# Moving the second half of a weight load from the sync queue to the ACT queue in the opening of a gated linear-attention and SwiGLU kernel

## The chip, the cores and the metric

The kernel runs on one core of one Trainium2 chip. The metric is the device time of a whole execution in microseconds; the span in a profile, from its first to its last instruction, is 1.7 us shorter.

Names: PE is TensorE's matmul, PEld its weight load, ACT ScalarE, DVE VectorE, POOL GpSimd, SP the sync engine, whose queue issues most DMAs. A q behind a name (ACTq, SPq) marks an entry of that engine's sequencer, such as the issue of a DMA.

## The reference, cut to what matters

```python
x = A_x                                       # 1 x 2048 x 512, bf16
g = sigmoid((x * gate_w).sum(-1, keepdims=True))
qkv = x @ wqkv                                # 512 x 1536: q, k, v; 32 heads of 16
pq, pk = phi(q), phi(k)                       # phi(t) = where(t > 0, t + 1, exp(t)) + 1e-6
kv, z = sum_s pk v, sum_s pk                  # per head, over ALL tokens
a = ((pq @ kv) / (pq . z + 1e-6)) @ wo
b = (silu(x @ w1) * (x @ w3)) @ w2            # 512 -> 1376 -> 512
out = g * a + (1 - g) * b
```

kv and z are sums over all tokens, so the kernel starts with k of all 16 token tiles, for which it needs wk and x transposed.

## The kernel before

The opening: x's first two token tiles come as rows and are transposed by PE; tiles 2 and 3 and all later ones come by transposing DMAs. wk (512 x 512) comes in two halves of 256 KB: chunks 0 and 1 of its rows, and chunks 2 and 3.

```python
dq = nc.sync
dq.dma_start(out=x_sb[:, 0:TF, :], in_=x_first)                                    # tiles 0, 1
nc.scalar.dma_start(out=wk_sb[:, 0:2, :], in_=wqkv_r[:, 0:2, D : 2 * D])           # first half
dq.dma_start(out=wk_sb[:, 2:4, :], in_=wqkv_r[:, 2:4, D : 2 * D])                  # second half
pre = consts.tile([1, 1], FP32, name="pre")
nc.scalar.activation(out=pre[:], in_=..., func=ACT.Exp)          # brings the table load with it
dq.dma_start(out=xT[:, :, TF * P : TB], in_=x2d[TF * P : TB, :], transpose=True)   # tiles 2, 3
for tb in range(1, NTB):
    dq.dma_start(out=xT[:, :, ...], in_=x2d[...], transpose=True)
    dq.dma_start(out=x_sb[:, x_ts, :], in_=x_r[:, x_ts, :])
# ... the other weights, all on the sync queue
emit_warm(TB, TB, TB, TB, TB, TB, P, P, P)      # 9 idle matmuls until x lands
emit_xT(0); emit_xT(1)                          # 8 transposes on PE; copies on DVE and ACT
for kc, t in ((0, 0), (1, 0), (0, 1), (1, 1), (2, 0), (3, 0)):
    emit_k_mm(k0[t], t, kc)                     # chunk kc of wk, token tile t
emit_k_phi(k0[0], 0)
for t in range(1, TPB):                         # the rest of tile 1, then tiles 2 and 3
    for kc in range(2 if t == 1 else 0, KC):
        emit_k_mm(k0[t], t, kc)
    emit_k_phi(k0[t], t)
# ... k of the other tiles, x^T pk, q, the FFN and the output: PE without a pause
```

The order of PE's work is fixed by the program. "Chunk 2" below is the fifth k matmul, the first to read wk's second half; "tile 2" is the ninth, the first to read the transposing load.

## Time and profile before

| | kernel before |
|---|---|
| time, median of 3 | 178.72 us (178.37 to 178.73) |
| span of the profiled execution | 176.2 us |
| PE busy, share of the chain that ended last | 98%, 96% |
| first half of wk: issue, landing | 0.80, 4.46 us (ACT queue) |
| second half of wk: issue, landing | 1.27, 5.29 us (sync queue) |
| transposing load of tiles 2 and 3: issue, landing | 1.73, 6.24 us (sync queue) |
| chunk 2 starts, tile 2 starts | 5.38, 6.28 us |

The table reads as follows. PE is the bound and runs from its first k matmul to its end with next to no idle time, so the time is set by when that run begins, by waits in its first few matmuls, and by what follows its end. The lines behind this, and how long chunk 2 and tile 2 wait for their data, are in the prediction.

### The profile page before, as it was taken

To read this page: it belongs to the slowest core of one execution; us is meant where nothing else is said; L and a number is where in the kernel's file an instruction comes from. 1 tells how busy PE (TensorE), PEld (TensorE's weight loads), DVE (VectorE), ACT (ScalarE), POOL (GpSimd) and SP (SyncE) were. 2 spreads that over 40 slices of the span, in tenths; PEclk is the share of its full clock that TensorE was granted. 3 is DMA by queue.
4 is the path that set the end of the run, shared out by engine and by line. 5 is a ranking of instruction groups with operands and counts; after the bars stand their busy time and mean duration, and the time that the engine had idled before them with its cause. 6 is when DMAs were issued, how large, how long until landed. Compare 5 with 4: busy or idle time off the path is not lost.

```text
span 176.2 us, 2619 instructions
## 1 busy us (share of the span) xinstructions
PE 172.6 (98%) x946; PEld 82.7 (47%) x946; DVE 117.5 (67%) x204; ACT 65.3 (37%) x123; POOL 67.0 (38%) x100
## 2 busy tenths in 40 slices
PE   7999999999999999999999999999999999999994
PEld 3444444464445454444454544444545444444463
DVE  0596857899998646697875466978754669776000
ACT  3624224475524333324243332333434323341222
POOL 7297655789028323282003232820032329100000
PEclk9999999999999999999999999999999999999999
DMA  4999989961003611126000101230002022300002
GB/s 164 241 281 222 266 249 364 355 197 24 9 0 81 50 40 34 37 61 91 0 0 7 60 18 51 57 79 2 0 11 67 7 67 55 65 0 4 30 30 60
DMA packets 30380, 15.14 MB, mean 86 GB/s; under 512 B 20928, under 2 KB 30240, under 8 KB 30368
## 3 DMA queue, kind: packets, MB, share of 16 engines
q1 hardware_dynamic: 29952, 14.67, 32.5%
q10 hardware_dynamic: 416, 0.31, 0.5%
q8 instruction: 7, 0.11, 0.3%
q14 instruction: 5, 0.04, 0.1%
HBM read 8.42 MB, written 2.10 MB: 60 GB/s over the span
## 4 chain that ended last, share of the span: by engine, by line
PE 96%; DMA 2%; DVE 0%; issue 0%
PE o_ps L383 20%; PE up_ps L341 20%; PE gate_ps L333 19%; PE o_ps L374 8%; PE q_ps L224 8%; PE XP L211 8%; PE k_ps L191 6%; PE r_ps L248 3%; PE k L191 2%; DMA wk_sb<-in_A_wqkv_dram 2%; PE o_ps L378 2%; PE gate L333 0%; PE kvT_ps L465 0%; PE W_ps L489 0%; DVE o_last L392 0%; PE gate L319 0%
## 5 line engine op out<-in xcount | busy, mean ns | idle before, releaser
L341 PE MATMUL up_ps<-xT,w_sb 128*128 128x512 bf16 x160 | 41.1, 379 | 0.0
L333 PE MATMUL gate_ps<-xT,w_sb 128*128 128x512 bf16 x156 | 40.0, 379 | 0.0
L232 POOL TENSOR_TENSOR qz<-pq,z_sb 128x512 f32<-128x512 bf16 x16 | 18.4, 1161 | 54.5 <-DVE pq L152 54.5
L346 ACT ACTIVATE th<-gate_ps 128x512 bf16<-128x512 f32 x39 | 23.3, 597 | 38.8 <-PE gate_ps L333 38.4
L383 PE MATMUL o_ps<-w_sb,hT 128*128 128x512 bf16 (+3 forms) x180 | 37.5, 355 | 0.0
L348 DVE SCALAR_TENSOR_TENSOR gs<-th,gate_ps 128x512 bf16<-128x512 bf16 x39 | 26.6, 683 | 5.9 <-ACT th L346 5.6
L353 DVE TENSOR_TENSOR hT<-up_ps,gs 128x512 bf16<-128x512 f32 x40 | 27.6, 691 | 3.5
L149 DVE TENSOR_SCALAR phi_m<-phi_e 128x512 bf16<-128x512 bf16 x32 | 13.6, 424 | 21.2 <-ACT phi_e L147 21.1
L383 PEld LDWEIGHTS <-hT 128*128 128x128 bf16 x180 | 16.8, 98 | 17.8
L301 POOL TENSOR_TENSOR pqn<-pq,rden 128x256 bf16<-128x256 bf16 x32 | 19.0, 625 | 15.9 <-DVE rden L292 14.8
L341 PEld LDWEIGHTS <-w_sb 128*128 128x128 bf16 x160 | 15.7, 98 | 18.9
L333 PEld LDWEIGHTS <-w_sb 128*128 128x128 bf16 x159 | 15.4, 98 | 18.5 <-issue 0.2
L388 ACT ACTIVATE o_out<-o_ps,omg 128x512 bf16<-128x512 f32 x15 | 10.3, 687 | 29.0 <-PE o_ps L383 26.3
L201 POOL TENSOR_TENSOR pks<-pks,pk_sb 128x512 f32<-128x512 f32 x15 | 17.5, 1164 | 7.4 <-DVE pk_sb L152 6.7
L374 PE MATMUL o_ps<-W_sb,pqT 128*128 128x512 bf16 (+3 forms) x72 | 16.8, 355 | 0.0
L224 PE MATMUL q_ps<-wq_sb,xT 128*128 128x512 bf16 x64 | 16.4, 379 | 0.0
L211 PE MATMUL XP<-pk_sb,x_sb 128*128 128x512 bf16 x64 | 16.3, 379 | 0.0
L235 DVE TENSOR_REDUCE den<-qz 128x32 f32<-128x512 f32 x16 | 11.0, 685 | 7.9 <-POOL qz L232 7.8
L147 ACT ACTIVATE phi_e<-k_ps 128x512 bf16<-128x512 f32 x12 | 7.2, 597 | 14.4 <-PE k_ps L191 14.4
L147 ACT ACTIVATE phi_e<-q_ps 128x512 bf16<-128x512 f32 x16 | 9.6, 597 | 7.8 <-PE q_ps L224 7.8
L191 PE MATMUL k_ps<-wk_sb,xT 128*128 128x512 bf16 x48 | 12.3, 379 | 0.0
L152 DVE SCALAR_TENSOR_TENSOR pq<-q_ps,phi_m 128x512 bf16<-128x512 f32 x16 | 11.1, 691 | 0.5
(66 smaller groups left out, 119.2 us busy)
## 6 DMA issues: line engine op xcount, KB each, us to landing
w_sb<-in_B_w_dram SPq DMA_DIRECT2D x4, 640.0 KB, 7.1
out_dram<-o_out SPq DMA_DIRECT2D x15, 128.0 KB, 1.7
w_sb<-in_B_w_dram SPq DMA_DIRECT2D x1, 1280.0 KB, 12.7
x_sb<-in_A_x_dram SPq DMA_DIRECT2D x2, 512.0 KB, 5.5
x_sb<-in_A_x_dram SPq DMA_DIRECT2D x1, 768.0 KB, 5.2
wq_sb<-in_A_wqkv_dram SPq DMA_DIRECT2D x1, 512.0 KB, 7.0
wv_sb<-in_A_wqkv_dram SPq DMA_DIRECT2D x1, 512.0 KB, 5.5
wo_sb<-in_A_wo_dram SPq DMA_DIRECT2D x1, 512.0 KB, 9.9
```

The source lines that it names most:

```text
L191: nc.tensor.matmul(k_ps[:], lhsT=xT[:, kc, t * P : (t + 1) * P], rhs=wk_sb[:, kc, :], start=(kc == 0), stop=(kc == KC - 1),)
L211: nc.tensor.matmul(XP_ps[dc][:], lhsT=x_sb[:, t, dc * P : (dc + 1) * P], rhs=pk_sb[:, t, :], start=(t == 0), stop=(t == NT - 1),)
L224: nc.tensor.matmul(q_ps[:], lhsT=xT[:, kc, ts_tok], rhs=wq_sb[:, kc, :], start=(kc == 0), stop=(kc == KC - 1),)
L232: nc.gpsimd.tensor_tensor(out=qz[:], in0=st[tb, "pq"][:, tt, :], in1=z_sb[:], op=ALU.mult)
L301: nc.gpsimd.tensor_tensor(out=pqn[:].rearrange("p (i c e) -> p c i e", i=NG, c=KC)[:, :, :, dsl], in0=st[tb, "pq"][:, tt, :].rearrange("p ...
L333: nc.tensor.matmul(gate_ps[:], lhsT=w1_sb[:, kc, fsl], rhs=xT[:, kc, tok_sl], start=(kc == 0), stop=(kc == KC - 1),)
L341: nc.tensor.matmul(up_ps[:], lhsT=w3_sb[:, kc, fsl], rhs=xT[:, kc, tok_sl], start=(kc == 0), stop=(kc == KC - 1),)
L346: nc.scalar.activation(out=th[:], in_=gate_ps[:], func=ACT.Tanh, scale=0.5)
L348: nc.vector.scalar_tensor_tensor(out=gs[:], in0=th[:], scalar=1.0, in1=gate_ps[:], op0=ALU.add, op1=ALU.mult)
L353: nc.vector.tensor_tensor(out=st[tb, "hT"][:, fc, :], in0=up_ps[:], in1=gs[:], op=ALU.mult)
L374: nc.tensor.matmul(o_ps[:], lhsT=st[tb, "pqT"][:, c, tsl], rhs=W_sb[:, c, a:b], start=(c == 0), stop=False,)
L383: nc.tensor.matmul(o_ps[:], lhsT=st[tb, "hT"][:, fc, tsl], rhs=w2_sb[:, fc, a:b], start=False, stop=(fc == FC - 1),)
```

## The change

Intent: the sync queue should not spend its second place on wk. wk's second half goes out on the ACT queue right behind its first half, ahead of the activation table's load, and the sync queue goes on at once with the transposing load, for which PE waits at tile 2.

```diff
     nc.scalar.dma_start(out=wk_sb[:, 0:2, :], in_=wqkv_r[:, 0:2, D : 2 * D])
-    dq.dma_start(out=wk_sb[:, 2:4, :], in_=wqkv_r[:, 2:4, D : 2 * D])
+    nc.scalar.dma_start(out=wk_sb[:, 2:4, :], in_=wqkv_r[:, 2:4, D : 2 * D])
     pre = consts.tile([1, 1], FP32, name="pre")
     nc.scalar.activation(out=pre[:], in_=nc.const_aps.tensor(0.0, [1, 1], FP32), func=ACT.Exp)
     dq.dma_start(
```

In the compiled program nothing else moves: PE, DVE and POOL have the same instructions in the same order, SP one fewer, ACT one more.

## The prediction

> **What bounds the kernel now.** I read the page's busy times and chain first, then the chain of the first 12 us in order of time, then the timeline of each engine there, then the DMA queues in short windows.
>
> ```profile
> PE 172.6 (98%) x946; PEld 82.7 (47%) x946; DVE 117.5 (67%) x204; ACT 65.3 (37%) x123; POOL 67.0 (38%) x100
> ...
> PE 96%; DMA 2%; DVE 0%; issue 0%
> ```
>
> TensorE is the bound: 172.6 of a span of 176.2 us, and 96% of the chain that ended last. The sums over one long window say how tight it is (columns: PE, PEld, DVE, ACT, POOL, each busy us and count, then clock, DMA share, GB/s):
>
> ```profile
> 4.51:173.60 169.09, 169.07 (x929) 81.12 (x929) 116.82 (x202) 63.60 (x121) 63.45 (x85) 1.00 0.33 85
> ```
>
> From its first k matmul to its last output matmul PE is idle for 0.02 us of 169.09, at full clock. (Matmul ends are modelled, so a short stall can hide in this sum; I look for those below.) There is nothing to win after the opening, and a delay before or in the first matmuls moves the end by as much. So the change is decided by the first 6.3 us. The chain there (start, us, what):
>
> ```profile
> 0.80 3.66 DMA wk_sb<-in_A_wqkv_dram
> 4.46 0.04 issue
> 4.51 3.67 PE k L191 x16
> ```
>
> It starts with the first half of wk, landing at 0.80 + 3.66 = 4.46. The 16 matmuls take 3.67 us, where 16 at the later pace (4 in 0.86 us, 0.216 each) would take 3.45. Part of the rest is the long end of the last one, and part a wait. The timeline of the weight loads shows which:
>
> ```profile
> 3.83 0.45 PEld L181 LDWEIGHTS <-x_sb 128*128 128x128 bf16 x8 [0.25 <-DMA x_sb<-in_A_x_dram]
> 4.50 1.41 PEld L191 LDWEIGHTS <-xT 128*128 128x128 bf16 x8 [0.22 <-DVE xT L186]
> 6.28 0.11 PEld L191 LDWEIGHTS <-xT 128*128 128x128 bf16 x2 [0.36 <-DMA xT<-in_A_x_dram]
> ```
>
> The third line is the wait that the change aims at: the matmuls of token tile 2 begin at 6.28, released by the transposing load. The matmul before started at 6.03, so the pace allowed 6.03 + 0.216 = 6.245. The wait is worth 0.03 to 0.04 us of PE's time; the 0.36 in the brackets is idle time of the weight loader, which idles 0.12 us before every load here anyway. The second line has no DMA wait between its eight loads: the matmuls of chunk 2, the first readers of wk's second half, start at 5.38, four paces after 4.51. That half was issued at 1.27 and took 4.0 us (its row of landings), so it landed at about 5.29, and PE reads it about 0.04 us after a landing (4.46 to 4.51). So it has under 0.1 us of slack.
>
> The issues on both queues and what ACT does meanwhile:
>
> ```profile
> 0.80 0.46 ACTq L86 DMA_DIRECT2D wk_sb<-in_A_wqkv_dram  x1
> 1.29 1.28 ACT L89 ACT_TABLE_LOAD   x1 [1.29 <-PEq L531]
> 4.27 0.38 ACT L188 ACTIVATE xT<-xTp 128x256 bf16<-128x256 bf16 x1 [1.48 <-PE xTp L181]
> ```
>
> ```profile
> 0.81 0.40 SPq L85 DMA_DIRECT2D x_sb<-in_A_x_dram  x1
> 1.27 0.41 SPq L87 DMA_DIRECT2D wk_sb<-in_A_wqkv_dram  x1
> 1.73 1.32 SPq L90 DMA_TRANSPOSE xT<-in_A_x_dram  x1
> ```
>
> Last, the queue table (packets, MB, share of 16 engines) of 2.9 to 3.7, of 4.1 to 4.45 and of 4.6 to 5.6 us; q10 is ACT's queue, q1 the sync engine's:
>
> ```profile
> q10 hardware_dynamic: 189, 0.19, 72.0%
> q1 hardware_dynamic: 56, 0.08, 27.4%
> ```
>
> ```profile
> q1 hardware_dynamic: 131, 0.13, 107.8%
> ```
>
> ```profile
> q1 hardware_dynamic: 1105, 0.28, 126.6%
> ```
>
> They give the cost of a packet: wk's 1 KB ones 1.078 x 16 x 0.35 us / 131 = 46 ns, the transposing load's 256 B ones 1.266 x 16 x 1.0 us / 1105 = 18 ns. A half of wk is 256 packets, 16 per DMA engine, 0.74 us; the transposing load is 256 KB, 1024 packets, 64 per engine, 1.17 us. Up to 2.9 us q1 alone moved packets (88 of them, x), then q10 for the most part, then q1 alone. So today x, wk's first half, its second half and the transposing load are served one after another, though the first two were issued at the same moment on two queues.
>
> **What the Trainium skill says.** "DMA: Bandwidth & Descriptors", section "Issuing engines are not separate DMA queues": DMAs of all engines run on the same 16 DMA engines and interleave; issuing from several saves the sequencer's time only. The trace agrees: the engines are full from 2.5 to beyond 6 us, so the order of service matters, not the number of queues. The same page, "Queues, rings and completion order", has each DMA engine go round its queues packet by packet. The trace does not show it for x and wk's first half, which hardly overlap. "Perfetto Trace Analysis", section "DMA Instruction — HWDGE (DVE, Sync)", gives a reason: the descriptor generator is one block that an issuing sequencer locks for exclusive use, and the recorded issue includes the wait for the lock. The trace fits loosely: ACT's issue took 0.46 us beside x's, the same transfer alone on SP 0.41. "TensorE: Matmul & The Clock Gate", part 1: the clock falls after about 3.4 us of idle time; a stall of 1 us should cost itself and no more (no row of this trace has one).
>
> **The change part by part.** Both programs hold the same instructions; the order on PE, DVE and POOL is the same, the waits too. One DMA moves from second on the sync queue to second on ACT's.
>
> Sync queue: 0.41 us and its gap go, so the transposing load is issued at 1.27 instead of 1.73, and all behind it 0.46 us earlier. Only the 0.04 us wait at 6.28 can be won. The next transposing load lands 4.9 us after 3.10 at the earliest (7.97), and its readers start at 8.88, so it is hidden already.
>
> ACT: the issue adds some 0.46 us; the table load goes from 1.29 to 1.75 and ends at 3.03, the dummy Exp (0.20) at 3.24. ACT's first real work starts at 4.27, so 1.03 us of slack is left. Cost 0.
>
> DMA engines: the same bytes, in another order. wk's second half and the transposing load are now ready within some 0.05 us of each other, around 1.27, and SP is free first (1.21 against 1.26). The first half of wk is asked for before both and should keep its place. What counts is the second half's landing, with under 0.1 us of slack.
>
> **The rivals.**
> (a) Served as before, wk's half ahead: the generator takes it between pieces of the long transposing issue. PE wins the wait at 6.28: -0.04 us. For it: only 0.05 us separates the two requests, and the 1.32 us issue may be many pieces.
> (b) Interleaved packet by packet: each of the 16 packets of wk waits for one of 18 ns, 16 x 18 = 0.29 us. The half lands at about 5.58 and chunk 2 starts at 5.62 instead of 5.38: +0.24 us. The wait at 6.28 is then hidden, so +0.2. If the first half is caught too, it comes 0.29 us later and the two delays add up to 0.4 or so. For it: two queues, one set of engines, and the skill's round robin.
> (c) The transposing load takes the generator for its whole 1.32 us, or its packets go first: the second half takes the last place and lands where the transposing load lands now, 1.73 + 4.5 = 6.23, or up to 5.29 + 1.17 = 6.46. Chunk 2 starts at 6.27 to 6.50: +0.9 to +1.1 us. ACT would be held till 2.59 and its table load would end near 4.3, with its first copy some 0.25 us late, which hides under the same stall (the copy is read at 5.38 at the earliest). For it: strict one-after-another service today, and SP being free first. Against it: ACT's issue beside x's grew by only 0.05 us.
> A fourth, that the earlier sync queue brings the later weights sooner, makes nothing: PE waits for no DMA after 6.28.
>
> **Range and chances.** The weights are a 0.3, b 0.4, c 0.3: 0.3 x (-0.04) + 0.4 x 0.3 + 0.3 x 0.95 = +0.39 us. The three runs before average 178.6 (178.37, 178.72, 178.73), so 179.0. The range is from 178.4, case (a) with a low run, to 179.8, case (c) with a usual one. 2% is 3.6 us, over three times the worst rival; 0.98 for within 2%, and slower a little likelier than faster.
>
> **What would show it.** In the changed profile the table load starts near 1.75 and ACT's first copy still at 4.27 (or near 4.5 under c). The transposing issue starts near 1.27. If the weight loads of the first k matmuls break at chunk 2 with a wait on wk, (b) or (c) is right, and its length tells which; then no wait is left on the transposing load. If chunk 2 still starts four paces after the first matmul and tile 2 follows in pace, it is (a). The landing of wk's first half, 3.7 us after issue, should hold within 0.1; if it grows the transposing load already mixes with that half. Wrong altogether would be an ACT copy that ends the wait at 5.38, or any idle time on PE after 6.5 us.

## The result, and the profile after

| | before | changed |
|---|---|---|
| median | 178.72 us (6 runs, 177.99 to 179.20) | 178.43 us (6 runs, 178.21 to 178.77) |
| ratio, 95% interval | | 0.999 (0.9965 to 1.0014) |

A ratio here is the mean time of one kernel's fast runs over that of the other's fast runs of the same rounds, so not quite the ratio of the medians quoted. The interval holds anything from 0.6 us won to 0.25 us lost.

The ACT and sync queues of the changed kernel (start, us, what), to set beside the issues of before:

```profile
0.80 0.47 ACTq L86 DMA_DIRECT2D wk_sb<-in_A_wqkv_dram  x1
1.30 0.50 ACTq L87 DMA_DIRECT2D wk_sb<-in_A_wqkv_dram  x1
1.82 1.28 ACT L89 ACT_TABLE_LOAD   x1 [1.82 <-issue]
3.12 0.20 ACT L89 ACTIVATE pre<-const-float32-0.0 1x1 f32<-1x1 f32 x1
4.35 0.81 ACT L188 ACTIVATE xT<-xTp 128x256 bf16<-128x256 bf16 x2 [1.03 <-PE xTp L181]
```

```profile
1.27 1.33 SPq L90 DMA_TRANSPOSE xT<-in_A_x_dram  x1
2.66 3.35 SPq L94 DMA_TRANSPOSE xT<-in_A_x_dram  x1
```

The intent was met at the issue: the transposing load goes out at 1.27 instead of 1.73, 0.03 us ahead of wk's second half. The table load moves by 0.53 us and ACT still idles 1.03 us before its first real work. The landings of that load, first in the kernel before, then in the changed one:

```profile
L90 SPq DMA_TRANSPOSE xT<-in_A_x_dram x1: 1324/1324/1324, 1.7 to 1.7; - x1
...
DMA to landing us min/median/max: 4.5/4.5/4.5
```

```profile
L90 SPq DMA_TRANSPOSE xT<-in_A_x_dram x1: 1335/1335/1335, 1.3 to 1.3; - x1
...
DMA to landing us min/median/max: 5.1/5.1/5.1
```

Issued 0.46 us earlier, it takes 0.6 us longer: it lands at 6.36 us, no earlier than before. What the DMA engines did in the meantime stands in the queue table of 3.75 to 4.25 us of the changed kernel (queue, packets, MB, share of 16 engines; q10 is ACT's queue, q1 the sync queue):

```profile
q10 hardware_dynamic: 178, 0.17, 106.2%
q1 hardware_dynamic: 1, 0.00, 0.2%
```

The engines are full with wk's second half, and the transposing load has moved one packet. The half went first although it was asked for last, by 0.03 us. In the 0.35 us after this window both queues move packets (78 of ACT's, 158 of the sync queue's). Then the weight loads of the opening, to set beside those of before:

```profile
3.69 0.78 PEld L181 LDWEIGHTS <-x_sb 128*128 128x128 bf16 x8
4.48 0.20 PEld L191 LDWEIGHTS <-xT 128*128 128x128 bf16 x2
4.96 0.15 PEld L191 LDWEIGHTS <-xT 128*128 128x128 bf16 x1 [0.28 <-DVE xT L186]
5.34 2.69 PEld L191 LDWEIGHTS <-xT 128*128 128x128 bf16 x13 [0.23 <-issue]
```

No DMA wait is left among them. But the reason isn't the change: here the loads take 0.15 us and stand 0.43 apart until 5.3 us, and the eight transposes take 0.78 instead of 0.45 us. PE ran at half its pace until then, while in the profile of before it had the full pace from 3.5 us on. Running late, it came to tile 2 at 6.42 and found its data there. So these two profiles can't be compared by their waits, and the experiments first had to deal with that.

One more line of each profile matters, the closing entries of the ACT queue (duration in ns, min/median/max; first and last start), before and changed:

```profile
L542 ACTq DRAIN  x2: 8/80/153, 174.0 to 175.8; - x2
```

```profile
L542 ACTq DRAIN  x2: 122/137/152, 174.4 to 176.4; - x2
```

The last drain takes 122 instead of 8 ns, and starts 2.7 instead of 2.4 us after PE's last weight load. From that weight load to the end of the span it is 2.83 us before and 3.03 in the changed kernel.

### The profile page after: what moved, and what is told of

It is laid out like the page before. It is cut to its first block, busy times and chain, and to the rows that moved or that the text cites. A ratio compares the mean times of both kernels' runs of the same rounds, so it can differ in the third digit from the quotient of the medians.

```text
span 176.7 us, 2603 instructions
## 1 busy us (share of the span) xinstructions
PE 172.1 (97%) x930; PEld 83.3 (47%) x946; DVE 117.5 (67%) x204; ACT 65.5 (37%) x123; POOL 67.1 (38%) x100
## 4 chain that ended last, share of the span: by engine, by line
PE 97%; issue 1%; DVE 0%
PE up_ps L341 20%; PE o_ps L383 19%; PE gate_ps L333 19%; PE o_ps L374 8%; PE q_ps L224 8%; PE XP L211 8%; PE k_ps L191 6%; PE r_ps L248 3%; PE k L191 2%; PE o_ps L378 2%; PE warm L168 2%; PE xTp L181 0%; PE gate L333 0%; PE kvT_ps L465 0%; PE W_ps L489 0%
```

## The experiments

Twelve kernels ran, in three sets of four, each set on one chip together with runs of the kernel before.

### 1. The kernel before against itself, and the changed kernel again

No edit. Both give another profile of the opening.

> The kernel before, unchanged, against itself. Theory O (the change does nothing, its 0.1% is scatter): ratio within 0.25% of 1, and runs of two kinds, with a recorded clock of 1.000 and of about 0.998, the second longer by 0.3 to 0.4 us (in the changed kernel's six runs: mean span 176.6 against 176.9 us). Theory G (the change wins a real 0.3 us): this kernel's runs agree with its own within 0.1 us and show no such two kinds. In the profile both expect the first half of wk to land at 4.2 to 4.6, the second half at 5.2 to 5.4 and the transposing load at 6.1 to 6.4 us.

> The changed kernel again. Theory O: ratio 0.998 to 1.002, the second half of wk lands at 5.2 to 5.4 us and the transposing load at 6.2 to 6.4 though it is issued near 1.27, so its issue to landing is about 5.0 us instead of 4.5. Theory G: ratio at or below 0.998 with the interval clear of 1, and the transposing load lands before 6.1 us.

Measured: the kernel before against itself 0.9977 (0.9943 to 1.0011), the changed kernel 1.0009 (0.9975 to 1.0044). So the 0.1% of the first result is less than what a kernel differs from itself. The recorded clock is not the mark of a kind of run that I expected: spans of 177.0 and of 176.2 both come with 1.000. The pace of the weight loads is a better one. In this second profile of the kernel before they are:

```profile
3.72 0.77 PEld L181 LDWEIGHTS <-x_sb 128*128 128x128 bf16 x8
4.50 0.20 PEld L191 LDWEIGHTS <-xT 128*128 128x128 bf16 x2
4.98 0.15 PEld L191 LDWEIGHTS <-xT 128*128 128x128 bf16 x1 [0.28 <-DVE xT L186]
5.41 0.15 PEld L191 LDWEIGHTS <-xT 128*128 128x128 bf16 x1 [0.28 <-issue]
5.83 0.15 PEld L191 LDWEIGHTS <-xT 128*128 128x128 bf16 x1 [0.28 <-issue]
6.26 0.15 PEld L191 LDWEIGHTS <-xT 128*128 128x128 bf16 x1 [0.28 <-issue]
6.69 1.20 PEld L191 LDWEIGHTS <-xT 128*128 128x128 bf16 x6 [0.28 <-issue]
```

One load each 0.43 us up to 6.7, then the full pace, and the span is 177.2 us. The four profiles so far give the full pace from 3.5, 5.3, 6.1 and 6.9 us on and spans of 176.2, 176.7, 177.1 and 177.2 us, in the same order, whichever of the two kernels it was. A microsecond at half pace costs up to half a microsecond of PE's work, less what PE would have waited for a landing anyway. "TensorE: Matmul & The Clock Gate" of the Trainium skill, part 1, says that the clock's monitor works in windows of about 3.4 us that don't start with the kernel, so that the moment varies from run to run; that fits.

The landings: the transposing load at 6.42 us in the kernel before and 6.14 in the changed one, so over two profiles each the means are 6.33 and 6.25 us, with 0.2 us between two executions of one kernel. wk's second half: 5.31 and 5.01. Two expectations for the changed kernel were missed: 6.2 to 6.4 for the transposing load by 0.06 us, and 5.2 to 5.4 for the half by 0.2. No gain of 0.46 us is there, and none of 0.3 us in the time.

### 2. The transposing load ahead of wk's second half on the sync queue

```diff
-    dq.dma_start(out=wk_sb[:, 2:4, :], in_=wqkv_r[:, 2:4, D : 2 * D])
 ...
     dq.dma_start(out=xT[:, :, TF * P : TB], in_=x2d[TF * P : TB, :], transpose=True)
+    dq.dma_start(out=wk_sb[:, 2:4, :], in_=wqkv_r[:, 2:4, D : 2 * D])
```

> Both loads on the sync queue, the transposing load ahead of wk's second half: this makes certain what rival (c) of the prediction supposed. Expected if the queue serves strictly in order and PE passes a late landing on to the end: the half lands at 6.2 to 6.5 us, the weight loads of chunk 2 wait about 0.8 to 1.1 us, time +0.8 to +1.1 us (ratio 1.0045 to 1.006). If a later clock rise or another wait already covers it: under +0.4 us. If the 1 KB packets overtake the 256 B ones on one queue: landing before 5.6 and a ratio of 1.

Measured: ratio 1.0048 (1.0016 to 1.0079), +0.86 us. The sync queue, and the row of the half that now comes second:

```profile
1.26 1.33 SPq L89 DMA_TRANSPOSE xT<-in_A_x_dram  x1
2.65 0.56 SPq L92 DMA_DIRECT2D wk_sb<-in_A_wqkv_dram  x1
```

```profile
  PE k L191: 1.3, 1
...
DMA to landing us min/median/max: 4.0/4.0/4.0
```

The half lands at 2.65 + 4.0 = 6.66 us, later than expected, because its issue has to wait for the 1.33 us of the other and its packets come slowly; PE waits 1.3 us for it, once. A late landing does pass on to the end, as the prediction's rival (c) had it. The same run answers the main question. The transposing load was issued at 1.26, as in the changed kernel, and landed at 5.30 instead of 6.14 to 6.36. Its queue table of 3.75 to 4.25 us:

```profile
q1 hardware_dynamic: 521, 0.13, 124.5%
q10 hardware_dynamic: 8, 0.00, 2.8%
```

In the stretch in which it moved one packet in the changed kernel it moves 521 packets here. So what held it back in the changed kernel was wk's second half on the other queue; experiment 4, which takes that half away, agrees. Where it was held back, at the DMA engines or earlier, where the descriptors of the transfers are made, no run tells apart: its first packet comes at 3.4 us here, with wk's first half still under way, and at 4.2 us in the changed kernel.

The half itself crawls here. Its 256 packets take from 4.5 to 6.2 us, 1.7 us, where the prediction's estimate for the half alone is 0.74. They share the one queue with packets of two transposing loads (4.45 to 6.2 us, both kinds together; wk's are 256 of the 779):

```profile
q1 hardware_dynamic: 779, 0.38, 113.3%
```

That is 0.38 MB in 1.75 us, about 217 GB/s, while the engines count as 113% busy.

### 3. wk's second half on ACT behind the table load

```diff
-    nc.scalar.dma_start(out=wk_sb[:, 2:4, :], in_=wqkv_r[:, 2:4, D : 2 * D])
     pre = consts.tile([1, 1], FP32, name="pre")
     nc.scalar.activation(out=pre[:], in_=..., func=ACT.Exp)
+    nc.scalar.dma_start(out=wk_sb[:, 2:4, :], in_=wqkv_r[:, 2:4, D : 2 * D])
```

> wk's second half on ACT behind the table load and the dummy Exp, issued near 2.8 us, well after the transposing load's issue at 1.27. Theory F (one generator, the transfers served in the order in which their requests reach it): the half comes behind the whole transposing load and lands at 6.2 to 6.6, time +0.8 to +1.2 us. Theory R (the DMA engines go round the two queues packet by packet): the half's 16 packets per engine alternate with the transposing load's, it lands 3.0 to 3.3 us after issue, at 5.8 to 6.1, and the transposing load at 6.2 to 6.4; time +0.4 to +0.7 us.

Measured: ratio 1.000 (0.9964 to 1.0036). It tested something else than I meant:

```profile
1.29 1.28 ACT L88 ACT_TABLE_LOAD   x1 [1.29 <-PEq L531]
1.36 0.43 ACTq L89 DMA_DIRECT2D wk_sb<-in_A_wqkv_dram  x1
```

The DMA goes out at 1.36 us, 0.07 us into the table load that stands before it in the program: ACT's sequencer issues it while the engine is still loading. So the place ahead of the table's load, which the change speaks of, is worth 0.06 us of issue time. The half landed at 1.36 + 4.1 = 5.45 us and the transposing load at 6.26, so the first half microsecond of reordering is given back here too. In the window of 3.75 to 4.25 us the transposing load moved 28 packets instead of 1. The half's request came 0.09 instead of 0.03 us after its own; that this made the difference isn't shown.

To put the half truly behind the table load, the dummy Exp then wrote an element of wk that the DMA overwrites, so that the DMA has to wait for it (edit against the run before):

```diff
-    pre = consts.tile([1, 1], FP32, name="pre")
-    nc.scalar.activation(out=pre[:], in_=..., func=ACT.Exp)
+    nc.scalar.activation(out=wk_sb[0:1, 2, 0:1], in_=..., func=ACT.Exp)
     nc.scalar.dma_start(out=wk_sb[:, 2:4, :], in_=wqkv_r[:, 2:4, D : 2 * D])
```

> Mends the run before this set: wk's second half truly behind the table load, because the dummy Exp writes a byte that it overwrites; issued near 2.8 us, 1.5 us after the transposing load. Theory F (served in order of request): lands at 6.2 to 6.7, PE waits at chunk 2 in every run, ratio 1.004 to 1.006 like the swap on the sync queue. Theory R (packet by packet between the two queues): lands at 5.8 to 6.1, ratio 1.001 to 1.004. The transposing load lands near 5.3 under F, at 5.6 or later under R.

Measured: two fast runs of 179.76 and 180.53 us (ratio 1.010, 1.006 to 1.0139), and four slow, up to 186.26. Both theories fall short. The profiled execution is one of the slow ones; the row of the half's issue at 2.83 us reads:

```profile
  PE k L192: 4.4, 1
...
DMA to landing us min/median/max: 8.0/8.0/8.0
```

The half took 8.0 us to land. Its packets ran beside the second transposing load (1024 packets for two tiles, twice that for four), and the two together moved little. Sums of that run (columns PE, PEld, DVE, ACT, POOL, then clock, DMA share, GB/s):

```profile
4.00:5.00 1.00, 1.00 (x9) 0.71 (x8) 0.58 (x2) 0.61 (x2) 0.62 (x2) 1.00 1.12 252
5.00:6.00 1.00, 1.00 (x4) 0.40 (x3) 0.00 (x0) 0.15 (x1) 0.00 (x0) 1.00 1.20 125
6.00:7.00 1.00, 0.41 (x2) 0.00 (x0) 0.00 (x0) 0.00 (x0) 0.00 (x0) 1.00 0.98 111
...
9.00:10.00 1.00, 0.00 (x0) 0.00 (x0) 0.00 (x0) 0.00 (x0) 0.00 (x0) 0.83 1.28 206
10.00:11.00 1.00, 0.17 (x1) 0.10 (x1) 0.00 (x0) 0.00 (x0) 0.00 (x0) 0.50 1.03 186
```

111 to 125 GB/s where the opening of the kernel before has 270 to 375, with the engines counted as busy as ever. While PE idled, the granted clock fell too (1.00, 0.83, 0.50), which goes with this run's counting as slow. The fast runs show that time is lost in every run (1.4 and 2.1 us over the median of before); how long the half crawls in those isn't shown, since only a slow one was profiled. Why a plain load and transposing ones slow each other like this stays open; experiment 2 has a milder case on one queue, so two queues aren't needed for it.

### 4. Without wk's second half (a wrong result)

```diff
-    dq.dma_start(out=wk_sb[:, 2:4, :], in_=wqkv_r[:, 2:4, D : 2 * D])
 ...
-            k_ps[:], lhsT=xT[:, kc, t * P : (t + 1) * P], rhs=wk_sb[:, kc, :],
+            k_ps[:], lhsT=xT[:, kc, t * P : (t + 1) * P], rhs=wk_sb[:, kc % 2, :],
```

> A wrong result on purpose: wk's second half is not loaded, chunks 2 and 3 read the first half. What it is worth to have its 256 KB out of the way. If the transposing load waits for the engines only because that half is ahead of it: it lands 0.7 to 1.0 us earlier (at 5.2 to 5.7) and PE never waits for it. Time: at most 0.1 us won when the clock rises early (PE is then bound by its start at 4.3 to 4.5), ratio 0.998 to 1.001. If the transposing load has a fixed delay of its own it lands at 6.1 to 6.4 as before.

Measured: ratio 0.9991 (0.9966 to 1.0017), relative error 0.027 as intended. The row of the transposing load's landing:

```profile
L89 SPq DMA_TRANSPOSE xT<-in_A_x_dram x1: 1313/1313/1313, 1.3 to 1.3; - x1
...
DMA to landing us min/median/max: 4.2/4.2/4.2
```

Issued at 1.26, it lands at 5.51: with those 256 KB out of the way it comes 0.6 to 0.9 us sooner. And still the time moves by less than the scatter. This bounds what an earlier landing of these two loads could win: the interval leaves at most 0.6 us, the wait at tile 2 in the first profile was worth 0.04 us, and in the other three profiles so far PE isn't even there yet when the load lands.

### 5. The opening held back until the clock is up

To see effects of 0.1 us the scatter had to go. In this pair five memsets on DVE (about 5.6 us) come first; one more writes an element of x and of wk, for which the first DMA on either queue has to wait. PE gets 19 idle matmuls instead of 9, the last four of them at 7.4 us, so that its clock is up and stays up. The two held-back kernels differ from each other in the change alone. (The compiler's scheduling is switched off for SP, ACT and DVE here, in both.)

```diff
+    for _ in range(5):
+        nc.vector.memset(hold[:], 0.0)                          # 128 x 1024 fp32
+    nc.vector.memset(xw_sb[0:1, 0 : NT + 1 : NT, 0:1], 0.0)     # x and wk are one tile here
+    nc.vector.memset(late_r[:], 1.0)
     dq.dma_start(out=x_sb[:, 0:TF, :], in_=x_first)
 ...
-    emit_warm(TB, TB, TB, TB, TB, TB, P, P, P)
+    emit_warm(*[TB] * 15)
+    warm_r = late_r[:]
+    emit_warm(TB, TB, TB, TB)
```

> The kernel before with its whole opening (all DMA issues) held back about 5.6 us by five memsets on VectorE, and PE kept busy meanwhile, so that its clock has risen before x lands. Theory K (the scatter of 1.5 us between runs comes from the moment at which the PE clock rises, 3.5 to 6.9 us into the span in the profiles so far): all matmuls of the opening run at 0.216 us, and the runs' spans lie within 0.4 us of each other instead of 176.0 to 177.7. If the scatter has another cause: they spread by over 1 us as before. Time +4.5 to +6.5 us over the kernel before in either case. Landings counted from the issue of x as in the kernel before: second half of wk 4.4 to 4.6, transposing load 5.3 to 5.7 us.

> The changed kernel held back in the same way; the only difference from the run above is the queue of wk's second half. Here the opening is bound by the transfers, so the change shows undiluted. Theory O (no effect: the half is served first on either queue): mean span within 0.1 us of the run above, the transposing load lands within 0.15 us of it counted from the issue of x. Theory L (in runs with an early clock rise the change costs 0.2 us: the shortest spans so far are 176.4 to 176.5 of the changed kernel against 176.0 to 176.3): mean span 0.1 to 0.3 us longer, with a longer wait on the transposing load or on wk. Theory G (a gain): 0.04 us or more shorter with no wait on the transposing load.

| held back | time of the runs, us | spans, us |
|---|---|---|
| kernel before | 183.76, 183.81, 183.82, 183.88 | 182.0 to 182.2, mean 182.10 |
| changed kernel | 184.03, 184.09, 184.13, 184.15, 184.19 | 182.3 to 182.5, mean 182.38 |

The scatter falls from 1.5 us to 0.12 and 0.16 us (0.2 to 0.6 in the three held-back kernels of the next set), so theory K holds for the most part: nearly all of it came from the moment at which PE's clock rises. And the two kernels separate: 184.118 against 183.817 us in the mean, 0.30 us or 0.16% more for the changed kernel, without overlap. The opening of the held-back kernel before, then of the changed one:

```profile
10.46 1.41 PEld L201 LDWEIGHTS <-xT 128*128 128x128 bf16 x8 [0.22 <-DVE xT L196]
12.19 0.76 PEld L201 LDWEIGHTS <-xT 128*128 128x128 bf16 x5 [0.32 <-DMA xT<-in_A_x_dram]
```

```profile
10.15 0.80 PEld L201 LDWEIGHTS <-xT 128*128 128x128 bf16 x5 [0.22 <-DVE xT L196]
11.31 0.53 PEld L201 LDWEIGHTS <-xT 128*128 128x128 bf16 x3 [0.36 <-issue]
12.25 0.76 PEld L201 LDWEIGHTS <-xT 128*128 128x128 bf16 x5 [0.41 <-DMA xT<-in_A_x_dram]
```

In the changed kernel x and wk's first half landed earlier in this execution (9.44 and 10.17 against 9.75 and 10.40 us), PE began earlier, waited for wk's second half (landed at 11.27) and again for the transposing load (12.21). Tile 2 starts at 12.25 against 12.19, a difference of 0.07 us. In the three held-back kernels of the next set it starts at 12.27 (before's order), 12.75 and 12.19 us (changed order), so 0.07 us is within the scatter between executions. That 0.07 us remains up to PE's last weight load (179.33 against 179.27), so PE lost nothing in between. But the spans of these two executions are 182.35 and 182.10. The other 0.18 us come after PE's end: from the last weight load to the end it is 3.02 us against 2.84. Looking back, that holds for every profile so far. Of the five profiles without a second load on ACT's queue four have 2.83 to 2.84 us (the one without wk's half has 2.91); all five with it have 3.01 to 3.03. The line that goes with it is the closing drain on ACT's queue, shown above for the first pair. For the held-back kernel before and the changed one it reads:

```profile
L552 ACTq DRAIN  x2: 8/80/152, 179.9 to 181.7; - x2
```

```profile
L552 ACTq DRAIN  x2: 121/137/153, 180.0 to 182.0; - x2
```

### 6. Is it the DMA or the instruction?

A second DMA on ACT's queue also makes ACT's stream of instructions one longer: 195 instead of 194 in the compiled program. Three held-back kernels tell the two apart, and one that is not held back. One instruction fewer, by moving an eviction of the third block from ACT to DVE:

```diff
+        if (tb, half) == (2, 1):
+            nc.vector.tensor_copy(out=upr[:], in_=r_ps[:, :, FR:NR])
+        else:
-        nc.scalar.activation(out=upr[:], in_=r_ps[:, :, FR:NR], func=ACT.Copy)
+            nc.scalar.activation(out=upr[:], in_=r_ps[:, :, FR:NR], func=ACT.Copy)
```

One more (in the kernel before) or three more (in the changed one), in the middle of the kernel:

```diff
+        for _ in range(1):          # 3
+            nc.scalar.activation(out=pre[:], in_=..., func=ACT.Exp)
```

> The held-back changed kernel with one ACT instruction fewer (one eviction of the third block moved to VectorE), so that ACT's stream is as long as before. Theory N (the 0.19 us that every kernel with a second load on ACT's queue took longer from its last weight load to its end comes from the one instruction more in ACT's stream): that tail is 2.83 us instead of 3.02, ACT's last drain takes 8 ns, mean span 182.1 to 182.25. Theory D (it comes from the second DMA on ACT's queue itself): tail 3.02 and span 182.4 as in the held-back changed kernel.

> The held-back kernel before with one dummy Exp on one element more on ACT, in the middle of the kernel where ACT has time; no DMA moved. Theory N: tail 3.02 us, ACT's last drain late by 0.28 us, mean span 182.3 (0.19 more than the 182.1 of the held-back kernel before). Theory D: tail 2.83 us, span 182.1.

> The held-back changed kernel with three dummy Exps more. Theory N in its narrower form (the last drain comes late only when it stands at a particular place in the stream, as at the start of a block of instructions that has to be fetched): tail 2.83 again or at another value, since the place has moved by three. In its wider form (any longer stream ends later): tail 3.02 or more. Theory D: tail 3.02.

> The changed kernel itself, not held back, with the one eviction on VectorE: does the change lose or win anything once ACT's stream is no longer than before? Theory N: tail 2.83 us, shortest spans 176.1 to 176.3 like the kernel before, ratio 0.997 to 1.002. Theory D: tail 3.02 us, shortest spans at 176.4 and above.

| | ACT instructions | last drain, ns | ACT's release to its last drain, us | last weight load to end, us |
|---|---|---|---|---|
| before, held back | 194 | 8 | 0.09 | 2.84 |
| before, one Exp more | 195 | 135 | 0.36 | 3.01 |
| changed, held back | 195 | 121 | 0.38 | 3.02 |
| changed, one eviction fewer | 194 | 8 | 0.09 | 2.85 |
| changed, three Exps more | 198 | 8 | 0.09 | 3.03 |
| changed, one fewer, not held back | 194 | 8 | 0.09 | 2.84 |

The lines for one Exp more in the kernel before, for one fewer in the changed one, and for three more:

```profile
L555 ACTq DRAIN  x2: 135/145/155, 180.0 to 182.0; - x2
```

```profile
L555 ACTq DRAIN  x2: 8/80/153, 180.6 to 182.3; - x2
```

```profile
L555 ACTq DRAIN  x2: 8/80/151, 179.9 to 181.9; - x2
```

The kernel before gets the late drain from one idle Exp, with no DMA moved, and the changed kernel loses it when its stream is as long as before: theory D falls. With three more the drain is on time too, so for the drain it is not "longer is slower" but one particular length: the narrow form of theory N. That kernel still ended as late, at 3.03 us: both its last stores took longer to land in this execution, ACT's 1.75 us instead of 1.53 to 1.55 in all others, the sync queue's 1.62 instead of 1.41 to 1.44.

The times follow less neatly, as landings in the opening scatter by 0.1 to 0.2 us even when held back. Mean times in this set: one more 184.22 us; one fewer 184.08 (with one run of 184.49); three more 184.01. One more is 0.18 us above the mean of the other two, where 0.19 was expected, but the runs overlap and the openings of the three differ (tile 2 above), so the times alone don't decide between N and D; the drain and the end after PE's last weight load do. Against the first held-back pair, which ran on another chip, each is 0.1 to 0.2 us higher than expected, so I compare only within a set. Not held back, one fewer gives 1.0009 (0.9987 to 1.003), shortest span 176.3 us, within what was expected but too coarse to show 0.19 us.

What happens at that place in the stream is shown in part. "Runtime: NRT & Kernel Launch" of the Trainium skill, section "Instruction fetch mechanics", says that instructions are fetched in blocks ahead of their use and calls the cost of crossing from one to the next mostly hidden. The traces do show fetches, as packets on instruction queues, and one of 8 KB (queue q14) moves with the length of ACT's stream. With 194 or 195 instructions it comes 3.3 to 3.7 us after PE's last weight load, behind the last instruction, in all 13 profiles. With 198 it comes already at 0.83 us, when the last two stores were on their way; from 180 to 181 us of that kernel:

```profile
q14 instruction: 1, 0.01, 3.2%
```

So a fetch falls close to the end of ACT's stream, and where it falls depends on the stream's length: behind the end with 195, ahead of the last drain with 198. That supports the explanation and doesn't prove it, since no run shows that with 195 the last drain waits for a fetch. The late stores of the kernel with 198 may have the same root, but that is one profile.

No run suggested a version that beats both kernels, and none was tried: without wk's second half at all the time does not fall measurably, and in the profile with the early clock the opening is in balance, with each load landing within 0.1 us of the matmul that needs it (landed and started: 4.46 and 4.51, 5.29 and 5.38, 6.24 and 6.28 us).

## Why the prediction was right or wrong

The measured 178.43 us lies at the lower end of the range from 178.4 to 179.8, and "within 2%" was right. Lying inside is partly luck: 178.43 is 0.03 us above the lower edge, and the median of one and the same kernel varies more than that between sets of runs (changed 178.43 and 178.83; before 178.0 to 178.72). The middle, 179.0, was 0.57 us above the measured median: +0.39 us had been forecast, and no difference was measured (0.999). Point by point it looks as follows.

- *The first 6.3 us decide, nothing after.* Right for PE: what a kernel has lost at tile 2 it still has lost at its last weight load. Wrong for the whole: 0.19 us of the change's cost lie after PE's end, where the prediction did not look.
- *The wait at tile 2 is worth 0.04 us, chunk 2 has under 0.1 us of slack.* Right for that execution, but it was one with an early clock. In three of the four profiles of the two kernels PE came too late to wait at all.
- *ACT pays 0.* Right in the opening: table load at 1.82 where 1.75 was expected, and the 1.03 us of slack are there to the hundredth. Wrong at the end: one instruction more delayed ACT's last drain by 0.28 us and the end by 0.19.
- *The rivals.* (a), the half first as before, was right about the order: the half lands at 5.0 to 5.3, the transposing load no earlier. Its gain of 0.04 us did not come, since it supposed that the load would lose its wait, and the load took back in transfer the 0.46 us that it had won in issue. (b), packet by packet, happened only in the last part of the half's transfer, and chunk 2 was not late for it. Its sum also takes the skill's packet for one row of 1 KB; the page means some 9 to 17 descriptors, and a half of wk has 16 rows for each DMA engine, so a half that goes in one piece is not against the page, and the 0.29 us does not follow from it. (c) did not happen either; its price, +0.9 to +1.1, was a little above the +0.86 us where the load is put first by force.
- *The step that failed* is the weighting: (b) and (c) had 0.7 of the chances and gave 0.12 + 0.285 = 0.405 us of the +0.39. What the runs put in its place is an opening with no shift that can be told from scatter (0.07 us in one pair of profiles) and 0.19 us at the end. The held-back pair has +0.30 us for both together; the runs that aren't held back can't resolve it (0.999 and 1.0009).
- *"SP is free first, by 0.05 us".* True (0.03 us in the profile), and it did not matter. These two were not served in the order of their issue. The transposing load's first packet comes 2.1 us after its issue in the swapped kernel (1.26 to 3.38 us), where only wk's first half was in its way; in the changed kernel the half's own first packet comes at 3.70. So being asked for first by 0.03 us gave the load nothing, and why the half's packets went ahead isn't shown. That the load's descriptors take longer to make is an explanation that I did not test.

## What to carry to other kernels

With the DMA engines full, moving a load to another queue changed here when its neighbour was asked for, not when it landed; ask whose packets it will pass, and check landings instead of issues. Before an effect of 0.1% is judged, find out what the scatter is made of: here holding the opening back until PE's clock was up cut it from 1.5 us to 0.2 us in the pair that mattered and turned "same" into 0.16% slower. And compare two traces to their very last entry: one instruction more on an idle engine went with 0.19 us lost after all the work was done, and an idle Exp in its place did the same.

## What the Trainium skill lacked or had wrong

- "DMA: Bandwidth & Descriptors", "Queues, rings and completion order": the page has each DMA engine go round its queues, a packet of some 9 to 17 descriptors at a time, but doesn't say what decides between two loads asked for at almost the same time. In the changed kernel ACT's queue moved 178 packets from 3.75 to 4.25 us and the sync queue 1, with a load issued at 1.27 us waiting in it; ahead of wk's half, that load moved 521 in the same stretch. The profile's packets are single rows of 1 KB, 16 for each engine, so this does not contradict the page; whether the waiting load's descriptors were ready by then no run shows. Its section "Issuing engines are not separate DMA queues" agrees with the first result: 0.46 us won in issue, and no earlier landing.
- No page has the crawl of a plain load beside transposing ones: 111 to 125 GB/s from 5 to 7 us and 8.0 us from issue to landing for 256 KB on two queues (one profile, slow), and 1.7 us for 256 packets on one queue (one profile, fast). The rules of "DMA: Bandwidth & Descriptors" say that a transpose next to ordinary DMAs needs nothing; that is said of the data being right, which they were, and leaves the time open.
- No page gives the case of a DMA behind a table load on ACT: it was issued at 1.36 us, the table load lasting from 1.29 to 2.57.
- "TensorE: Matmul & The Clock Gate", part 1, gives 500 ns either way for the moment at which the clock rises, and adds that the count of slow matmuls varies from run to run. Here the full pace came at 3.5 to 6.9 us, with the first matmul at 0.84 in each case, a spread of 3.4 us. The page's warning that the clock's records can be wrong agrees: they say 1.00 for stretches in which the matmuls stood 0.43 us apart.
- "Runtime: NRT & Kernel Launch", "Instruction fetch mechanics": no page warns that the length of an engine's stream can show in the time. 195 instructions on ACT instead of 194 delayed its last drain by 0.27 to 0.29 us and the end by 0.17 to 0.20. With 198 the drain was on time and the end as late as with 195 (one profile).
